# One step of the token mixing ahead of the last projections, and three of the last four normed blocks written by ScalarE

## The chip, the cores and the metric

The kernel runs on one core of a Trainium2 chip. The metric is the device time of one launch in microseconds (us). The engines are TensorE (PE in the profile, with PEld for its weight loads), VectorE (DVE), ScalarE (ACT), GpSimd (POOL) and SyncE (SP), whose queue issues nearly all DMAs.

## The reference

The sequence has S = 2048 tokens of width D = 512, in bfloat16. First an attention block with 32 heads of width 16 and a causal window of 256 tokens, then a token mixing: an MLP that runs along the sequence, with F = 1792 hidden units. Both are modulated by six vectors made from a condition `c`. Cut to what matters:

```python
sa, ca, ga, sb, cb, gb = split((silu(c) @ w_mod), 6)
h = layernorm(x) * (1 + ca) + sa
x = x + ga * (attention(h, wqkv) @ wo)         # sliding window
h = layernorm(x) * (1 + cb) + sb
h = layernorm(h)
u = gelu(einsum('bsd,sf->bdf', h, w1) + b1)    # contracts over tokens
y = einsum('bdf,fs->bds', u, w2) + b2
x = x + gb * transpose(y)
```

Because the first mixing product contracts over tokens, every one of its outputs needs the twice normed rows of all 2048 tokens.

## The kernel before

The 2048 rows are 16 row blocks of 128 tokens (`tb`, 0 to 15), in four groups of four. The kernel has three stages.

The first stage is the attention, which lasts to about 163 us of the span. Its work is a set of tasks on all engines, put in order at build time by a planner (class `Order`) from a list of ranks (`PLACE`) and estimated costs; the order of each engine's instructions is then fixed. In it the output projection and both layernorms of row blocks 0 to 11 are done too, giving `hb[0]` to `hb[11]`, and as a filler a part of the first mixing product: for the ten chunks of 128 hidden units in `PART` (4 to 13) the sums over row blocks 0 to 7 are made, and copied from PSUM to SBUF as `part[fc]` (L1177, on DVE, from one of two PSUM banks `bk`). The half of w1 for row blocks 0 to 7 is in SBUF (`w1a`) by then.

The second stage, the tail, is the one that the change touches. It is written out by hand inside `tc.manual_schedule()`, so that each engine runs its instructions in the order of the code (L1249 to L1297). It makes row blocks 12 to 15:

- `t_wo(tb)`: the projection, four matmuls into a bank `pa` of the pool `ps_big` (two banks, the ones that `bk` had), and the addition to the residual on DVE (L1255, L1259).
- `t1(tb)`: statistics for the first layernorm, `t_stats`: two DVE operations (`stats_of`, L447 and L448), then two on POOL for one over the standard deviation (`rstd_of`, L440 and L442).
- `t2(tb)`: the first layernorm applied (`t_apply`, L1268), times `bc_cb1` (L1279), plus `bc_sb` (L1280), all on DVE, and statistics of the result.
- `t3(tb)`: the second layernorm applied with `t_apply`, which writes `hb[tb]`.

The steps are skewed: in one pass of the loop the blocks 12 + step, 11 + step and 10 + step are at `t1`, `t2` and `t3`. Between the projections stand steps of the first mixing product: `emit_b1_group0_sc(sc)` adds row block `sc` to the hidden chunks 0 to 5, in six PSUM banks `pu0` and `pu1`, which are those that the attention's scores had. For `sc` below 8 that is four matmuls (chunks 4 and 5 have these rows in `part`), from 8 on it is six, with weights `w1b` (L1234). After the loop stand the remaining row blocks to 15. Row block `sc` needs `hb[sc]`.

`load_rest(done)` issues, on SP's queue, the eight loads of `w1b` (the other half of w1) and the fourteen of `w2r`; the first waits for the last matmul of the first projection in the tail, since it writes memory that the attention used.

The third stage is dense: hidden chunks 6 to 13 (L1318), Gelu on ACT (L1245, with an addition of `part` on DVE, L1243), the second mixing product (L1344) and the output (L1351, L1356, L1357).

Of the kernel before, what the change touches and what calls it, by code (L numbers as in the profile page):

```python
# [8 lines left out]
DT = mybir.dt  # L9
ACT = mybir.ActivationFunctionType  # L10
ALU = mybir.AluOpType

P = 128
# [5 lines left out]
NT = S // P  # L19
# [245 lines left out]
def kernel(  # L265
# [14 lines left out]
    nc = tc.nc  # L280
# [157 lines left out]
    def rstd_of(var, n, name):  # L438
        ve = small.tile([P, n], DT.float32, name=name + "_ve")
        nc.gpsimd.tensor_scalar(out=ve[:], in0=var, scalar1=EPS, scalar2=0.0, op0=ALU.add, op1=ALU.add)  # L440
        r = small.tile([P, n], DT.float32, name=name)
        nc.gpsimd.tensor_tensor(out=r[:], in0=ve[:], in1=mhalf[:, 0:n], op=ALU.pow)  # L442
        return r

    def stats_of(src, mv):
        stats = small.tile([P, nc.vector.BN_STATS_DIM], DT.float32, name="stats")
        nc.vector.bn_stats(out=stats[:], in_=src)  # L447
        nc.vector.bn_aggr(out=mv, in_=stats[:])  # L448
# [49 lines left out]
    with tc.manual_schedule():  # L498
# [26 lines left out]
        shift = small.tile([P, 1], DT.float32, name="shift0")  # L525
# [11 lines left out]
        for n, c0 in ((0, MF), (1, MO)):  # L537
            nc.scalar.activation(
                out=mask_q[:, 128 * n : 128 * n + 128].rearrange("p (a b) -> p a b", a=2),
                in_=rows[:, c0 : c0 + 64].unsqueeze(1).to_broadcast([P, 2, 64]), func=ACT.Copy,  # L540
# [78 lines left out]
        for par, lo, hi in ((0, 192, 512), (1, 0, 512), (0, 0, 192)):  # L619
            nc.vector.tensor_scalar(  # L620
                out=QP[0][:, par, lo:hi], in0=first[0][:, lo:hi], scalar1=mask_par[:, par : par + 1], scalar2=0.0,
                op0=ALU.mult, op1=ALU.add,
# [587 lines left out]
    def load_rest(after):  # L1210
        for sc in range(NT - NA):
            load = dma.dma_start(out=w1b[:, sc, :], in_=w1_v[:, NA + sc, :])
            if sc == 0:
                later_than(load, after)
        for fc in range(NF):
            dma.dma_start(out=w2r[:, fc, :], in_=w2_v[:, fc, :])

    def w1_of(sc, fc):
        w = w1box["a"][:, sc, :] if sc < NA else w1b[:, sc - NA, :]
        return w[:, fc * P : (fc + 1) * P]  # L1220
# [8 lines left out]
    def emit_b1_group0_sc(sc):  # L1229
        for gi, pu in ((0, pu0), (1, pu1)):  # L1230
            for i, fc in enumerate(fgroups[gi]):
                s0 = 8 if fc in PART else 0
                if sc >= s0:
                    nc.tensor.matmul(  # L1234
                        pu[:, i, :], lhsT=w1_of(sc, fc), rhs=hb[sc][:],
                        start=(sc == s0), stop=(sc == NT - 1),
                    )
# [11 lines left out]
    with tc.tile_pool(name="xp2", bufs=4) as xp2, tc.manual_schedule():  # L1249
        v = {}  # L1250

        def t_wo(tb):
            pa = ps_big.tile([P, D], DT.float32, name="pa")
            for g in range(ND):
                mm = nc.tensor.matmul(  # L1255
                    pa[:], lhsT=OT[12 + g][:, (tb - 12) * P : (tb - 11) * P], rhs=wod[:, g, :],
                    start=(g == 0), stop=(g == ND - 1),
                )
            nc.vector.tensor_tensor(out=xres[tb][:], in0=pa[:], in1=xres[tb][:], op=ALU.add)  # L1259
            return mm.ins.name  # L1260

        def t_stats(src, key):
            v[key] = xp2.tile([P, nc.vector.BN_AGGR_DIM], DT.float32, name="ln2_mv")
            stats_of(src, v[key][:])
            v[key, "r"] = rstd_of(v[key][:, 1:2], 1, "ln2")

        def t_apply(out, src, key):
            nc.vector.tensor_scalar(  # L1268
                out=out, in0=src, scalar1=v[key][:, 0:1], scalar2=v[key, "r"][:],
                op0=ALU.subtract, op1=ALU.mult,  # L1270
            )

        def t1(tb):
            t_stats(xres[tb][:], (2, tb))

        def t2(tb):
            h2 = v["h", tb] = xp2.tile([P, D], DT.bfloat16, name="h2")
            t_apply(h2[:], xres[tb][:], (2, tb))
            nc.vector.tensor_tensor(out=h2[:], in0=h2[:], in1=bc_cb1[:], op=ALU.mult)  # L1279
            nc.vector.tensor_tensor(out=h2[:], in0=h2[:], in1=bc_sb[:], op=ALU.add)  # L1280
            t_stats(h2[:], (3, tb))

        def t3(tb):
            t_apply(hb[tb][:], v["h", tb][:], (3, tb))

        for step in range(6):
            if step < 4:
                done = t_wo(12 + step)
                if step:
                    emit_b1_group0_sc(step - 1)  # L1290
                else:
                    load_rest(done)
            for f, n in ((t1, step), (t2, step - 1), (t3, step - 2)):
                if 0 <= n < 4:
                    f(12 + n)
        for sc in range(3, NT):
            emit_b1_group0_sc(sc)  # L1297

    ps_big.release()
# [28 lines left out]
    with tc.tile_pool(name="ftmp", bufs=3) as ftmp, tc.tile_pool(  # L1328
        name="ps_y0", bufs=4, space=PSUM
    ) as ps_y0, tc.tile_pool(name="ps_y1", bufs=4, space=PSUM) as ps_y1:  # L1330
        for tg in range(NT // 4):
# [16 lines left out]
            for tl, lo, hi in parts:  # L1348
# [3 lines left out]
                    out=o1[:, lo:hi], in0=pys[4 if lo else tl][:, lo:hi], scalar=b2FM[:, tb : tb + 1], in1=bc_gb[:, lo:hi],  # L1352
                    op0=ALU.add, op1=ALU.mult,
# [35 lines left out]
```

## Time and profile before

| | us |
|---|---|
| timed runs | 250.66, 251.11, 253.0 (median 251.11) |
| the profiled execution | 251.63 |
| its span, first to last instruction | 249.9 |
| busy: PE, DVE, ACT, POOL | 240.5, 168.1, 157.7, 125.2 |
| attention stage, about | 0 to 163 |
| tail, to the last L1234 | 163 to 184 |
| dense stage to the last matmul | 184 to 246.5 |

The profile has one row for each instruction or group, with its start, its duration, the engine, the line of the code, the tile written and the tiles read. In square brackets stands how long the engine was idle before it and what ended that idle time. "PE pa L1255 <- DVE part L1177" in the view of waits means that PE, at line 1255, waited for line 1177 on DVE. Matmuls overlap in the array: one of 512 columns is shown at 0.38 us, while their starts lie closer together, so the cost of a matmul is read from the distance of starts.

### The profile page before, as it was taken

To read this page: it belongs to the slowest core of one execution; us is meant where nothing else is said; L and a number is where in the kernel's file an instruction comes from. 1 tells how busy PE (TensorE), PEld (TensorE's weight loads), DVE (VectorE), ACT (ScalarE), POOL (GpSimd) and SP (SyncE) were. 2 spreads that over 40 slices of the span, in tenths; PEclk is the share of its full clock that TensorE was granted. 3 is DMA by queue.
4 is the path that set the end of the run, shared out by engine and by line. 5 is a ranking of instruction groups with operands and counts; after the bars stand their busy time and mean duration, and the time that the engine had idled before them with its cause. 6 is when DMAs were issued, how large, how long until landed. Compare 5 with 4: busy or idle time off the path is not lost.

```text
span 249.9 us, 10602 instructions
## 1 busy us (share of the span) xinstructions
PE 240.5 (96%) x4710; PEld 126.5 (51%) x4710; DVE 168.1 (67%) x324; ACT 157.7 (63%) x183; POOL 125.2 (50%) x228
## 2 busy tenths in 40 slices
PE   8999999989999999999999999989999999999994
PEld 2644745545654555655554664544444444444443
DVE  7686879869997978787958686679824404251544
ACT  5467999999999999999999999200056300000000
POOL 5536952980299999869894997724400000000000
PEclk9999999999999999999999999999999999999999
DMA  6935554332460444211201010059999000201121
GB/s 202 325 106 152 149 140 137 108 76 77 121 201 3 97 121 114 74 34 23 42 10 37 18 22 3 3 164 390 415 410 384 6 0 5 81 28 56 42 88 42
DMA packets 25490, 28.14 MB, mean 113 GB/s; under 512 B 10212, under 2 KB 22628, under 8 KB 25444
## 3 DMA queue, kind: packets, MB, share of 16 engines
q1 hardware_dynamic: 25148, 27.20, 34.8%
q8 instruction: 37, 0.61, 1.0%
q10 hardware_dynamic: 296, 0.26, 0.3%
q14 instruction: 9, 0.07, 0.1%
HBM read 22.03 MB, written 2.10 MB: 97 GB/s over the span
## 4 chain that ended last, share of the span: by engine, by line
PE 72%; ACT 14%; DVE 5%; POOL 3%; DMA 3%; issue 2%; SPq 0%; ACTq 0%; POOLq 0%
PE py L1344 19%; ACT et L734 13%; PE bk L473 11%; PE bk L477 8%; PE pu L1234 7%; PE bk L759 6%; PE pu L1318 6%; PE pss L716 5%; PE bk L504 3%; PE pss L688 2%; PE pss L724 2%; PE pa L1255 1%; DMA VU<-V 1%; DMA x<-in_A_x_dram 1%; PE pss L697 1%
## 5 line engine op out<-in xcount | busy, mean ns | idle before, releaser
L734 ACT ACTIVATE et<-pss 128x1024 bf16<-128x1024 f32 x152 | 140.6, 1062 | 3.4 <-PE pss L724 3.3
L1344 PE MATMUL py<-guT,w2r 128*128 128x512 bf16 (+1 forms) x238 | 48.5, 367 | 0.0
L1344 PEld LDWEIGHTS <-w2r 128*128 128x128 bf16 x238 | 23.2, 98 | 25.4
L1351 DVE SCALAR_TENSOR_TENSOR o<-py,bFM,bc_gb 128x512 bf16<-128x512 f32 (+1 forms) x17 | 11.7, 717 | 30.5 <-PE py L1344 30.5
L781 POOL TENSOR_TENSOR merge<-t,zr 128x512 bf16<-128x512 f32 x16 | 17.4, 1084 | 19.4 <-DVE zr L777 19.4
L768 DVE STREAM_TRANSPOSE t<-bk 128x512 f32<-128x512 f32 x32 | 22.6, 710 | 6.6 <-PE bk L759 5.4
L716 PE MATMUL pss<-QP,KT 32*128 32x192 bf16 (+2 forms) x672 | 25.6, 236 | 0.9 <-ACT et L734 0.5
L913 POOL TENSOR_SCALAR QP<-QR,mask_par 128x512 bf16<-128x512 bf16 x30 | 21.6, 724 | 7.7 <-DVE QR L626 4.7
L716 PEld LDWEIGHTS <-KT 32*128 32x128 bf16 x672 | 13.4, 92 | 18.2 <-issue 14.0
L473 PE MATMUL bk<-h1T,wqkv 128*128 128x512 bf16 x76 | 20.4, 382 | 0.3 <-ACT h1T L602 0.3
L759 PE MATMUL bk<-et,V 128*32 128x64 bf16 (+2 forms) x704 | 19.3, 240 | 0.4 <-DVE V L933 0.3
L759 PEld LDWEIGHTS <-V 128*32 128x32 bf16 x704 | 14.7, 96 | 7.8 <-issue 4.2
L724 PE MATMUL pss<-mask_q,mask_k 32*128 32x64 bf16 (+2 forms) x496 | 18.3, 213 | 0.0
L1245 ACT ACT_TABLE_LOAD x1 | 1.3, 1283 | 26.0 <-issue 26.0
L1243 DVE TENSOR_TENSOR gelu_a<-pu,part 128x512 f32<-128x512 f32 x10 | 6.5, 687 | 11.5 <-PE pu L1318 8.7
L1124 POOL TENSOR_TENSOR h<-h,bc_sb 128x512 bf16<-128x512 bf16 x12 | 13.9, 1155 | 0.6
L1318 PE MATMUL pu<-hb,w1b 128*128 128x512 bf16 x64 | 14.0, 379 | 0.0
L724 PEld LDWEIGHTS <-mask_k 32*128 32x128 bf16 x496 | 13.3, 93 | 0.4
L933 DVE CAST V<-bk 128x512 bf16<-128x512 f32 x16 | 11.1, 691 | 3.5 <-PE bk L477 1.5
L477 PE MATMUL bk<-h1T,wqkv 128*32 128x512 bf16 x192 | 12.7, 382 | 0.0
L759 PE MATMUL bk<-et,VU 128*32 128x64 bf16 x448 | 11.8, 194 | 0.9 <-DMA VU<-V 0.9
L759 PE MATMUL bk<-et,VL 128*32 128x64 bf16 x512 | 12.2, 193 | 0.0
(138 smaller groups left out, 406.0 us busy)
## 6 DMA issues: line engine op xcount, KB each, us to landing
w2r<-in_B_w_dram SPq DMA_DIRECT2D x14, 512.0 KB, 10.2
w1a<-in_B_w_dram SPq DMA_DIRECT2D x16, 224.0 KB, 3.2
w1b<-in_B_w_dram SPq DMA_DIRECT2D x8, 448.0 KB, 7.2
wmod<-in_w_mod_dram SPq DMA_DIRECT2D x8, 256.0 KB, 3.0
out_dram<-otile SPq DMA_DIRECT2D x15, 128.0 KB, 1.7
x<-in_A_x_dram SPq DMA_DIRECT2D x14, 128.0 KB, 3.1
VL<-V SPq DMA_DIRECT2D x15, 96.0 KB, 2.8
VU<-V SPq DMA_DIRECT2D x27, 48.0 KB, 2.4
```

The costliest lines, as they stand in the source:

```text
L473: nc.tensor.matmul(out, lhsT=lhsT, rhs=rhs, start=start, stop=stop, skip_group_check=True)
L477: nc.tensor.matmul(out[cols, :], lhsT=lhsT[:, cols], rhs=rhs, start=start, stop=stop, tile_position=(0, 32 * j), skip_group_check=True,)
L716: mm(pss[j // 2][:, j % 2, c0 : c0 + nq], lhsT=keys(4 * tg + kb)[rows[j], :], rhs=QP[s][rows[j], par, q0 : q0 + nq], start=n == 0, stop=False,
L724: mm(pss[j // 2][:, j % 2, c0 : c0 + hi - lo], lhsT=mask_k[rows[j], 0:P], rhs=mask_q[rows[j], lo:hi], start=False, stop=n + 1 == len(masks ...
L734: e = nc.scalar.activation(out=et[:], in_=held.pop(("pss", u, a))[:], func=ACT.Exp, scale=SCORE_SCALE)
L759: nc.tensor.matmul(po[32 * j : 32 * j + 32, q0 : q0 + nq], lhsT=v(j), rhs=held["et", s, k, j // 2][:, j % 2, c0 : c0 + nq], start=n == 0, ...
L768: nc.vector.transpose(out=held["t2", s][:, par, :], in_=psum.pop(("po", s, par))[:])
L781: nc.gpsimd.tensor_tensor(out=m[:].rearrange("p (b a d) -> p a b d", a=2, d=DH), in0=t2v(s, 0, DH, DH), in1=held["zr", s][:].to_broadcast( ...
L913: nc.gpsimd.tensor_scalar(out=QP[s][:, par, :], in0=QR[s][:], scalar1=mask_par[:, par : par + 1], scalar2=0.0, op0=ALU.mult, op1=ALU.add,)
L1234: nc.tensor.matmul(pu[:, i, :], lhsT=w1_of(sc, fc), rhs=hb[sc][:], start=(sc == s0), stop=(sc == NT - 1),)
L1318: nc.tensor.matmul(pu[:, i, :], lhsT=w1_of(sc, fc), rhs=hb[sc][:], start=(sc == s0), stop=(sc == NT - 1),)
L1344: nc.tensor.matmul(pys[4 if lo else tl][:, lo:hi], lhsT=w2r[:, fc, tb * P : (tb + 1) * P], rhs=guT[fc][:, lo:hi], start=(fc == 0), stop=(f ...
```

## The change

Two things are changed in the tail.

One step of L1234, that of row block 0, is put ahead of the loop, so ahead of the first projection. The steps in the loop then go one row block further each (1, 2, 3 in place of 0, 1, 2), and the rest begins at 4. The number of matmuls is the same. `load_rest` stays behind the first projection.

For row blocks 12, 13 and 14, the second layernorm (key 3) is applied by ScalarE, as an `Identity` activation with scale r and bias -mean * r. The bias is made by two operations of 128 x 1 on GpSimd, right behind those of `rstd_of`. Block 15 is still written by VectorE.

```diff
+        def by_scalar(key):
+            return key[0] == 3 and key[1] < NT - 1
+
         def t_stats(src, key):
             v[key] = xp2.tile([P, nc.vector.BN_AGGR_DIM], DT.float32, name="ln2_mv")
             stats_of(src, v[key][:])
-            v[key, "r"] = rstd_of(v[key][:, 1:2], 1, "ln2")
+            r = v[key, "r"] = rstd_of(v[key][:, 1:2], 1, "ln2")
+            if by_scalar(key):
+                shift = v[key, "shift"] = xp2.tile([P, 1], DT.float32, name="ln2_sh")
+                nc.gpsimd.tensor_scalar(
+                    out=shift[:], in0=v[key][:, 0:1], scalar1=-1.0, scalar2=0.0, op0=ALU.mult, op1=ALU.add,
+                )
+                nc.gpsimd.tensor_tensor(out=shift[:], in0=shift[:], in1=r[:], op=ALU.mult)
 
         def t_apply(out, src, key):
+            if by_scalar(key):
+                nc.scalar.activation(
+                    out=out, in_=src, func=ACT.Identity, bias=v[key, "shift"][:], scale=v[key, "r"][:],
+                )
+                return
             nc.vector.tensor_scalar(
                 out=out, in0=src, scalar1=v[key][:, 0:1], scalar2=v[key, "r"][:],
                 op0=ALU.subtract, op1=ALU.mult,
...
+        for sc in range(1):
+            emit_b1_group0_sc(sc)
         for step in range(6):
             if step < 4:
                 done = t_wo(12 + step)
                 if step:
-                    emit_b1_group0_sc(step - 1)
+                    emit_b1_group0_sc(step + 0)
                 else:
                     load_rest(done)
             for f, n in ((t1, step), (t2, step - 1), (t3, step - 2)):
                 if 0 <= n < 4:
                     f(12 + n)
-        for sc in range(3, NT):
+        for sc in range(4, NT):
             emit_b1_group0_sc(sc)
```

## The prediction

> **What bounds the kernel now.** I read the page's busy shares first, then TensorE (PE) in stretches around the change, then its waits there, then the chain that ended last.
>
> ```profile
> span 249.9 us, 10602 instructions
> ...
> PE 240.5 (96%) x4710; PEld 126.5 (51%) x4710; DVE 168.1 (67%) x324; ACT 157.7 (63%) x183; POOL 125.2 (50%) x228
> ...
> core 0: us, PE busy (x) PEld busy (x) DVE busy (x) ACT busy (x) POOL busy (x), PEclk, DMA share, GB/s
> 162.65:163.42 0.77, 0.00 (x1) 0.00 (x1) 0.69 (x1) 0.00 (x0) 0.00 (x0) 1.00 0.00 0
> 163.42:184.13 20.71, 20.71 (x96) 9.38 (x96) 15.38 (x36) 0.12 (x1) 7.19 (x16) 1.00 0.91 349
> 184.13:197.95 13.82, 13.82 (x66) 6.24 (x65) 5.16 (x8) 8.69 (x13) 0.00 (x0) 1.00 0.69 275
> 197.95:246.50 48.55, 48.54 (x239) 23.14 (x237) 17.69 (x34) 1.33 (x2) 0.00 (x0) 1.00 0.12 41
> ```
>
> The third to fifth numbers of a stretch are busy times. PE stands still for the 0.77 us from 162.65 to 163.42, and from there to 246.5 it has no gap at all, at granted clock 1.00. ScalarE (ACT) is idle until 184, VectorE (DVE) is busy 15.38 of 20.71 us.
>
> ```profile
> PE pa L1255 <- DVE part L1177: 0.8, 1, 0.8
> ...
> 158.99 3.66 PE bk L477 x64
> ...
> 162.67 0.70 DVE part L1177
> ...
> 163.42 1.89 PE pa L1255 x8
> ```
>
> The first row is PE's only wait after 156 us, the others are from the chain in order of time. The last partial product of the first stage ends at 162.65; DVE copies its PSUM bank out; only then may the projection of block 12 (L1255) write that bank. That is the hole. Everything after it is a row of matmuls whose number the change leaves alone, so the end moves by what happens to the hole, unless an operand comes late.
>
> **Edit one: one step of L1234 ahead of the projections.** PE's order in the built kernel differs in one thing: four L1234 matmuls of row block 0 stand ahead of the first L1255, and each later step stands one place earlier. Nothing is added. These four write the PSUM banks of the score tiles, not the bank that DVE empties, and read a block and weights from long before.
>
> ```profile
> 162.55 0.10 PEld L1255 LDWEIGHTS <-OT 128*128 128x128 bf16 x1 [0.42 <-issue]
> ...
> 168.59 5.34 PE L1234 MATMUL pu<-hb,w1a 128*128 128x512 bf16 x24
> 173.77 10.52 PE L1234 MATMUL pu<-hb,w1b 128*128 128x512 bf16 x48
> 184.13 2.11 PE L1318 MATMUL pu<-hb,w1b 128*128 128x512 bf16 x9
> ...
> 154.19 3.78 ACT L734 ACTIVATE et<-pss 128x1024 bf16<-128x1024 f32 x4
> 184.01 1.28 ACT L1245 ACT_TABLE_LOAD   x1 [26.04 <-issue]
> ```
>
> The first weights of the next stage are already loaded at 162.55 to 162.65, so the four can start at 162.65. Their banks were last read by ACT's exponentials, which end at 154.19 + 3.78 = 157.97. A matmul step costs (184.13 - 173.77) / 48 = 0.2158 us, four cost 0.86: they fill the hole of 0.77 and push the projection from 163.42 to 162.65 + 0.86 = 163.51, 0.09 late. PE's total is unchanged, so all PE work from 163.51 on has the hole behind it: gain 163.42 - 162.65 = 0.77 us. Bounds: 0, if the four cannot start early, and 0.79, the wait as rounded in its row.
>
> What is late next: blocks 12 to 15 start 0.09 later while their consumers come 0.77 earlier. On the new clock the first w1b step (row block 8) begins at 173.00, and blocks 12, 13, 14, 15 (24, 30, 36, 42 steps on) are wanted at 178.18, 179.47, 180.77 and 182.06.
>
> ```profile
> 164.51 4.40 SPq L1212 DMA_DIRECT2D w1b<-in_B_w_dram  x8
> 169.02 15.52 SPq L1216 DMA_DIRECT2D w2r<-in_B_w_dram  x14
> ...
> DMA to landing us min/median/max: 4.7/7.2/8.3
> ```
>
> The w1b loads are released by the end of block 12's projection, so they too start 0.09 later, at 164.60. Even at the longest landing of the eight, 8.3, the first is there at 172.90, against 173.00; at 4.7, which I take, since it goes out with nothing ahead of it, at 169.3. Later ones are issued some 0.55 apart and wanted 6 x 0.2158 = 1.29 apart, so their margin only grows. Cost 0.
>
> **Edit two: three of the four last blocks written by ScalarE.** DVE loses three applies; GpSimd (POOL) gains three pairs of 128x1 operations (the shift); ACT gains three activations. No queue of DMAs is touched by it.
>
> ```profile
> 164.48 0.69 DVE L1259 TENSOR_TENSOR x<-pa,x 128x512 bf16<-128x512 f32 x1 [1.11 <-PE pa L1255]
> ...
> 168.04 0.42 DVE L1279 TENSOR_TENSOR h<-h,bc_cb 128x512 bf16<-128x512 bf16 x1
> ...
> 173.47 0.38 DVE L1268 TENSOR_SCALAR hb<-h,ln_mv,ln 128x512 bf16<-128x512 bf16 x1
> 173.76 0.69 DVE L1259 TENSOR_TENSOR x<-pa,x 128x512 bf16<-128x512 f32 x1
> ...
> 177.47 0.38 DVE L1268 TENSOR_SCALAR hb<-h,ln_mv,ln 128x512 bf16<-128x512 bf16 x1
> 177.77 0.41 DVE L1268 TENSOR_SCALAR h<-x,ln_mv,ln 128x512 bf16<-128x512 bf16 x1
> ...
> 179.86 0.18 DVE L448 BATCH_NORM_AGGREGATE ln_mv<-stats 128x2 f32<-128x6 f32 x1
> ...
> 181.10 0.41 DVE L1268 TENSOR_SCALAR hb<-h,ln_mv,ln 128x512 bf16<-128x512 bf16 x1 [0.76 <-POOL ln L442]
> ```
>
> On DVE, block 12's apply was worth 173.76 - 173.47 = 0.29 to what follows, block 13's 177.77 - 177.47 = 0.30, and block 14's nothing, because DVE then waited 0.76 for POOL anyway. With the 0.09 delay, DVE stands at -0.20 after the first removal and -0.50 after the second. Block 15 is then ready at 181.10 - 0.50 + 0.41 = 181.01, wanted at 182.06: 1.05 to spare. Without edit two it would be 181.60, still 0.46 early.
>
> ```profile
> 168.17 0.72 POOL L442 TENSOR_TENSOR ln<-ln_ve,mhalf 128x1 f32<-128x1 f32 x1
> ...
> 170.27 0.56 POOL L442 TENSOR_TENSOR ln<-ln_ve,mhalf 128x1 f32<-128x1 f32 x1
> ...
> 174.02 0.56 POOL L442 TENSOR_TENSOR ln<-ln_ve,mhalf 128x1 f32<-128x1 f32 x1
> 175.48 0.29 POOL L440 TENSOR_SCALAR ln_ve<-ln_mv 128x1 f32<-128x1 f32 x1 [0.90 <-DVE ln_mv L448]
> ...
> 178.02 0.57 POOL L442 TENSOR_TENSOR ln<-ln_ve,mhalf 128x1 f32<-128x1 f32 x1
> ...
> L442 POOL TENSOR_TENSOR ln<-ln_ve,mhalf 128x1 f32<-128x1 f32 x8 | 5.0, 622 | 0.7
> ...
> L468 POOL TENSOR_TENSOR fours<-fours 128x4 f32<-128x4 f32 x9 | 2.2, 240 | 0.7
> ...
> L602 ACT ACTIVATE h1T<-pss,modFM 128x512 bf16<-128x512 bf16 x1 | 0.8, 777 | 2.6 <-PE pss L579 2.6
> ```
>
> A shift pair costs between 2 x 0.24 (L468, the same multiply on a small tile) and 2 x 0.62 (L442, a power), plus some 0.16 between; I take 0.64, the nearer kind, and keep 1.40. An ACT apply costs 0.78 (L602: the same function with scale and bias from memory), and I allow 0.1 before it. Block 12: power ends 170.92, pair 171.56, ACT 172.44, wanted 178.18. Block 13: 174.67, 175.31, 176.19, wanted 179.47. Block 14: 178.59 - 0.20 = 178.39, 179.03, 179.91, wanted 180.77; with the dear pair 180.67, still in time. Behind block 13's pair on POOL waits block 15's first square root: it could begin at 175.48 - 0.20 = 175.28, and with the dear pair begins at 176.07 and ends by 177.16, while DVE wants it at 177.27. The built order shows one more wait, of the last L442 for ScalarE; even if that were for block 14's write, at 179.91 it is over before 180.00, when that L442 is due. Behind ACT's applies stand only the table load and the Gelus, which at 184.01 - 0.77 = 183.24 wait for PE as before. Edit two alone moves no end: worth 0, hidden behind the weights stream and block 15's spare time.
>
> The Trainium skill speaks against this edit in two places. "SBUF — State Buffer", section "SBUF: two separate sides", says that VectorE and GpSimd take a shared port pair exclusively, one operation blocking the other. The trace agrees: L442 took 0.72 at 168.17, beside L1279 with two SBUF inputs, against 0.56 at 170.27. By that rule every shift operation beside such a DVE operation waits it out; the first rival prices this from the rows. "ScalarE: Activation LUTs", section "Rules for kernel authors", would leave a multiply and add on VectorE; by the trace that is 0.78 against 0.38 per apply, and the spare time of block 14 pays it.
>
> **Sum.** The profiled execution took 251.63, of which 249.9 is the span. 251.63 - 0.77 + 0 + 0 = 250.86. It lies 0.52 above the median of the three timed runs (250.66, 251.11, 253.0), so against the median 251.11 - 0.77 = 250.3.
>
> **Rivals.**
>
> 1. *The hole moves to a late block.* POOL's pairs beside DVE, or the power behind them, make block 14 or 15 late. For: block 14 has only 0.86 to spare, 0.10 with the dear pair. Against: blocks 12 and 13 have 5.7 and 3.3, and to eat the whole gain block 14 would have to slip 0.86 + 0.77. L442 takes 0.72 - 0.56 = 0.16 more beside L1279 than alone; if both shift operations stretch so and the pair is dear, block 14 is 0.2 late: 250.5. All of the gain back: 251.1. Chance 0.07.
> 2. *The four don't fill the hole.* If the first L1234 waits for the same copy, projection and blocks come 0.86 late and PE ends as before: 251.1, no gain. Against: no wait stands on it in the built order, and its banks are free since 157.97. Chance 0.07.
> 3. *Slower: ScalarE's new instructions are not at hand.* The page has queues that carry instructions, sharing the DMA engines, and from 166 on these are full.
>
> ```profile
> q14 instruction: 9, 0.07, 0.1%
> ...
> w2r<-in_B_w_dram SPq DMA_DIRECT2D x14, 512.0 KB, 10.2
> ```
>
> If ScalarE's next instructions had to be fetched behind these loads when block 12 is due (171.66), at 10.2 us, as a w2r load, block 12 would be written at 182.64 instead of 172.44; PE would stand 4.5 us at row block 12: 251.1 - 0.77 + 4.5 = 254.8. It decides from a delay of 5.74 + 0.77 = 6.5 us. Against: ScalarE is idle from 157.97, with time to fetch before the loads start, and its built order has no table load ahead of the three. Chance 0.04.
>
> **How the numbers follow.** Forecast 0.80 at 250.3; rivals 0.07, 0.07 and 0.04; 0.02 for runs that scatter further than those shown. The range goes from the fastest run less the gain, 250.66 - 0.79 = 249.9, less 0.2 because three runs hardly show the fastest, to the profiled run without any gain, 251.6, and 0.1 on top: 249.7 to 251.7. One per cent, 2.5 us, is about what a measurement of this kernel tells from no change. Forecast and rivals 1 and 2 lie within it: 0.93. Slower: rival 3 and a scatter like the run at 253.0, 0.05. Faster: 0.02, there is no second hole to fill.
>
> **What would show it.** Right: four L1234 rows from 162.65, the projection at 163.5, no PE wait from there on, row block 8 at 173.0, L1318 at 183.4, L1344 at about 197.2; ScalarE applies near 171.7, 175.4 and 179.1 at 0.78 each; block 15 on DVE near 180.6. Wrong: a PE wait on ACT or DVE at L1234 between 178 and 183 (rival 1), the first L1234 after 163.4 (rival 2), a long idle stretch of ACT past 172 with its sources ready (rival 3), or a w1b step that waits for a DMA at 173.

## The result and the profile after

The changed kernel takes 249.78 us (median of 20 runs, 249.07 to 251.65) against 251.12 (20 runs, 249.96 to 253.0). The ratio is 0.9947, with a 95% interval of 0.9926 to 0.9968: 0.8 to 1.9 us less. Forecast were 250.3 and a gain of 0.77. All ratios leave out single executions that ran over 1.5% longer than the fastest of their kernel (one of the reordering alone, one of four steps on VectorE), and they need not equal the quotient of the two medians.

The chain in order of time, of the changed kernel (start, duration, what):

```profile
157.83 3.64 PE bk L477 x64
161.47 0.16 issue
161.62 0.81 PE pu L1234 x3
162.44 1.73 PE pa L1255 x8
164.16 0.86 PE pu L1234 x4
```

The copy by VectorE (L1177) no longer stands in the chain. The row "issue" with three matmuls behind it is a missing record of the first of four. In a second profile of the same kernel all four are there. Its PE rows, from the timeline (start, duration, engine, line):

```profile
158.98 3.64 PE L477 MATMUL bk<-hb,w1a 128*32 128x512 bf16 x64
...
162.55 1.04 PE L1234 MATMUL pu<-hb,w1a 128*128 128x512 bf16 x4
163.42 1.89 PE L1255 MATMUL pa<-wod,OT 128*128 128x512 bf16 x8
...
172.92 10.52 PE L1234 MATMUL pu<-hb,w1b 128*128 128x512 bf16 x48
183.28 7.07 PE L1334 MATMUL pu<-hb,w1b 128*128 128x512 bf16 x32
```

This execution reached the last filler 0.01 us from where the profile of before did (158.99), so the two can be laid over each other. The projection begins at 163.42 in both. The dense stage (L1318 before, now L1334) begins at 183.28, not 184.13: 0.85 us earlier, or 0.84 from the filler on. The dense stage itself is unchanged: to the end of the last matmul it lasts 62.4 us in the kernel before and in the changed one.

The second edit, in the first profile after: GpSimd's power and pair for block 14, with the VectorE operation beside the power, then ScalarE's three applies and VectorE's last one.

```profile
176.49 0.43 DVE L1293 TENSOR_TENSOR h<-h,bc_cb 128x512 bf16<-128x512 bf16 x1
...
176.62 0.71 POOL L442 TENSOR_TENSOR ln<-ln_ve,mhalf 128x1 f32<-128x1 f32 x1
177.40 0.19 POOL L1271 TENSOR_SCALAR ln_sh<-ln_mv 128x1 f32<-128x1 f32 x1
177.67 0.19 POOL L1274 TENSOR_TENSOR ln_sh<-ln_sh,ln 128x1 f32<-128x1 f32 x1
...
170.25 0.81 ACT L1278 ACTIVATE hb<-h,ln_sh,ln 128x512 bf16<-128x512 bf16 x1 [13.43 <-DVE ln_mv L448]
173.93 0.81 ACT L1278 ACTIVATE hb<-h,ln_sh,ln 128x512 bf16<-128x512 bf16 x1 [2.87 <-POOL ln_sh L1274]
177.90 0.81 ACT L1278 ACTIVATE hb<-h,ln_sh,ln 128x512 bf16<-128x512 bf16 x1 [3.16 <-POOL ln_sh L1274]
...
179.31 0.41 DVE L1282 TENSOR_SCALAR hb<-h,ln_mv,ln 128x512 bf16<-128x512 bf16 x1 [1.00 <-POOL ln L442]
...
182.13 8.15 PE L1334 MATMUL pu<-hb,w1b 128*128 128x512 bf16 x36
```

A row block of L1234 is six matmuls, 1.295 us, so PE wants block 15 at 182.13 - 1.295 = 180.84, block 14 at 179.54. The two are written by 179.72 and 178.71: 1.12 and 0.83 us early. The three activations queue without a table load: ScalarE's only one in the tail still belongs to the Gelus.

### The profile page after: what moved, and what is told of

It is laid out like the page before. It is cut to its first block, busy times and chain, and to the rows that moved or that the text cites. A ratio compares the mean times of both kernels' runs of the same rounds, so it can differ in the third digit from the quotient of the medians.

```text
span 247.9 us, 10575 instructions
## 1 busy us (share of the span) xinstructions
PE 235.4 (95%) x4673; PEld 125.3 (51%) x4710; DVE 167.1 (67%) x321; ACT 160.0 (65%) x186; POOL 126.7 (51%) x234
## 4 chain that ended last, share of the span: by engine, by line
PE 72%; ACT 14%; DMA 4%; issue 3%; DVE 3%; POOL 2%; SPq 1%; ACTq 0%
PE py L1360 19%; ACT et L734 14%; PE bk L473 11%; PE bk L477 9%; PE pu L1234 7%; PE bk L759 6%; PE pu L1334 6%; PE pss L716 5%; PE pss L688 2%; PE pss L724 2%; DMA x<-in_A_x_dram 2%; DMA VU<-V 1%; PE pa L1255 1%; PE pss L697 1%; POOL xn L451 1%
## 5 line engine op out<-in xcount | busy, mean ns | idle before, releaser
L1360 PE MATMUL py<-guT,w2r 128*128 128x512 bf16 (+1 forms) x234 | 48.3, 366 | 0.2
L1360 PEld LDWEIGHTS <-w2r 128*128 128x128 bf16 x238 | 23.3, 98 | 25.3
L473 PE MATMUL bk<-h1T,wqkv 128*128 128x512 bf16 x65 | 18.5, 382 | 1.0 <-issue 0.5
L1278 ACT ACTIVATE hb<-h,ln_sh,ln 128x512 bf16<-128x512 bf16 x3 | 2.4, 813 | 19.5 <-DVE ln_mv L448 13.4
L1334 PE MATMUL pu<-hb,w1b 128*128 128x512 bf16 x62 | 13.9, 379 | 0.1
L477 PE MATMUL bk<-h1T,wqkv 128*32 128x512 bf16 x192 | 12.7, 381 | 0.0
L906 DVE CAST QR<-bk 128x512 bf16<-128x512 f32 x14 | 9.6, 687 | 4.0 <-PE bk L473 2.8
L900 DVE CAST KT<-bk 128x512 bf16<-128x512 f32 x15 | 10.3, 686 | 2.7 <-PE bk L473 1.2
```

What stands on the lines that cost most here:

```text
L473: nc.tensor.matmul(out, lhsT=lhsT, rhs=rhs, start=start, stop=stop, skip_group_check=True)
L477: nc.tensor.matmul(out[cols, :], lhsT=lhsT[:, cols], rhs=rhs, start=start, stop=stop, tile_position=(0, 32 * j), skip_group_check=True,)
L1334: nc.tensor.matmul(pu[:, i, :], lhsT=w1_of(sc, fc), rhs=hb[sc][:], start=(sc == s0), stop=(sc == NT - 1),)
L1360: nc.tensor.matmul(pys[4 if lo else tl][:, lo:hi], lhsT=w2r[:, fc, tb * P : (tb + 1) * P], rhs=guT[fc][:, lo:hi], start=(fc == 0), stop=(f ...
```

## The experiments

All times of the tail below are from the first of the 64 L477 matmuls to the first matmul of the dense stage: 184.13 - 158.99 = 25.14 before, 182.13 - 157.83 = 24.30 in the changed kernel.

**The reordering alone.** Against the changed kernel:

```diff
-            return key[0] == 3 and key[1] < NT - 1
+            return False
```

> The reordering alone: one L1234 step ahead of the projections, all four last blocks still written by VectorE. Hole theory (the gain is the filled hole of 0.85 us from matmul start to matmul start, nothing else): from the first L477 of the last filler (64 in a row) to the first matmul of the dense stage 24.30 us, as in the changed kernel, against 25.14 before; no PE wait in the tail; block 15 written 0.46 us and block 14 0.34 us before PE wants them; time 0.85 below the kernel before. Rival (the ScalarE half carries the part of the measured 1.33 that the hole does not explain): 24.3 us plus a wait at L1234 near the last blocks, and a time 0.5 us above that of the changed kernel.

249.96 us (12 runs) against 250.66; ratio 0.9952 (0.9926 to 0.9977). PE in the tail:

```profile
157.84 3.64 PE L477 MATMUL bk<-hb,w1a 128*32 128x512 bf16 x64
...
182.14 4.05 PE L1334 MATMUL pu<-hb,w1b 128*128 128x512 bf16 x17
```

24.30 us. VectorE wrote block 14 at 179.21 and block 15 at 180.38, 0.34 and 0.47 us before PE wanted them. The reordering has the whole gain of the tail.

**The ScalarE half alone.** The order of the matmuls is put back:

```diff
-        for sc in range(1):
-            emit_b1_group0_sc(sc)
...
-                    emit_b1_group0_sc(step + 0)
+                    emit_b1_group0_sc(step - 1)
...
-        for sc in range(4, NT):
+        for sc in range(3, NT):
```

> ScalarE writes blocks 12 to 14, the order of the matmuls is that of before. Hole theory: the hole of 0.8 us stays, tail 25.14 us from the first L477 of the last filler to the dense stage, time as before within 0.3 us. Rival (the ScalarE half carries 0.5 us): 250.6 where before has 251.1.

251.28 us against 250.66; ratio 1.0018 (0.9994 to 1.0043). The tail is 184.99 - 159.85 = 25.14 again, with the same hole:

```profile
159.85 3.64 PE L477 MATMUL bk<-hb,w1a 128*32 128x512 bf16 x64
164.28 1.89 PE L1255 MATMUL pa<-wod,OT 128*128 128x512 bf16 x7 [0.79 <-DVE part L1177]
...
184.99 1.24 PE L1332 MATMUL pu<-hb,w1b 128*128 128x512 bf16 x5
```

Worth nothing by itself, as forecast.

**The other bank first.** The kernel before, with the two PSUM banks of the fillers kept, and handed to the projections in the order in which VectorE empties them:

```diff
-            pa = ps_big.tile([P, D], DT.float32, name="pa")
+            pa = bank((tb + 1) % 2)
```

> The order and the engines of before, but the projections take the two PSUM banks in the other order: block 12 the one that was emptied earlier, block 13 the one that VectorE empties last. Hole theory (the hole is the wait for that one bank): block 12's projection starts as soon as the last filler is through, block 13's 0.86 us later, when the copy has just ended (0 to 0.1 us of wait); tail 24.3 to 24.4 us, time 0.75 to 0.85 below before, without any reordering and with ScalarE idle. Rival (the hole is PE's own change from 32-column to 128-column matmuls, or the wait for the last transposed attention block OT, and the four L1234 matmuls only happen to fit in it): the hole stays, 25.1 us, time as before.

249.82 us against 250.66; ratio 0.9962 (0.9937 to 0.9987).

```profile
158.78 3.64 PE L477 MATMUL bk<-hb,w1a 128*32 128x512 bf16 x64
162.35 1.90 PE L1252 MATMUL bk<-wod,OT 128*128 128x512 bf16 x7
...
183.08 3.19 PE L1316 MATMUL pu<-hb,w1b 128*128 128x512 bf16 x13
```

The projection starts 3.57 us after the first L477, as the four L1234 matmuls do in the changed kernel, and the tail is 24.30. So the hole was the wait for that bank and nothing else: it can be filled with other work, or not be made.

**Two steps ahead, with and without ScalarE.** `range(2)` in the changed kernel, the later steps one further; then the same with all four blocks on VectorE (one execution, 250.09 us against a median of 250.77).

> The changed kernel with two L1234 steps ahead of the projections, not one. Hole theory: the hole is already full, a second step gains nothing; projections and blocks come 0.86 us later while PE wants them at the same time, so block 14, 0.83 us early in the changed kernel, becomes 0.03 to 0.15 late; tail 24.30 + 0.03 to 0.15 us, time as the changed kernel within 0.2. Rival (more independent work ahead is better, there is more to fill than the hole): a further gain of up to 0.8 us.

> Two L1234 steps ahead of the projections, and all four last blocks written by VectorE (no ScalarE half). Spare-time theory (the ScalarE half is only cover: it brings blocks 14 and 15 earlier by about 0.5 us, which counts only where they would be late): block 14, 0.34 us early with one step ahead, is 0.52 us late with two, so PE waits about 0.5 to 0.6 us for VectorE at row block 14 of L1234, and the tail from the first L477 of the last filler to the dense stage is 24.30 + 0.5 to 0.6 = 24.8 to 24.9 us, against 24.39 with the ScalarE half. Rival (spare times read from the profile are not reliable to 0.3 us, or the ScalarE half is worth nothing anywhere): 24.4 us as with it.

With ScalarE the tail is 181.86 - 157.47 = 24.39 (249.53 us against 250.66; ratio 0.9969, 0.9944 to 0.9994): no second hole, and block 14 is 0.09 late. Without it the tail is 182.59 - 157.72 = 24.87:

```profile
171.66 7.93 PE L1234 MATMUL pu<-hb,w1b 128*128 128x512 bf16 x35
180.01 2.75 PE L1234 MATMUL pu<-hb,w1b 128*128 128x512 bf16 x12 [0.41 <-DVE hb L1282]
182.59 7.72 PE L1334 MATMUL pu<-hb,w1b 128*128 128x512 bf16 x34
```

PE waits at row block 14, 36 matmuls into the row (35 are recorded), for VectorE. From start to start the hole is 180.01 - (171.66 + 36 x 0.2158) = 0.58; the bracket says 0.41, since a matmul's row reaches past the point where the next may start. So the ScalarE half is worth 0.48 us, in this kernel and not in the changed one.

**Four steps ahead, with and without ScalarE.** `range(4)`, the later steps three further.

> Four L1234 steps ahead of the projections, with the ScalarE half. Spare-time theory: blocks come 3 x 0.863 = 2.59 us later than in the changed kernel, block 14 had 0.83 us to spare, so PE waits 1.76 to 1.85 us for ScalarE at row block 14; tail 24.30 + 1.8 = 26.1 us, slower than before (25.14) by 0.9 us; the w1b loads, released 2.59 us later, still land in time if the first takes the shortest landing of 4.3 us. Rival (the first w1b load takes the longest landing of 8.5 us): a wait of 2.7 us for a DMA at row block 8, and none at row block 14; tail 27.0 us.

> Four L1234 steps ahead of the projections, all blocks written by VectorE. Spare-time theory: block 14 is 2.25 us late (0.34 - 2.59), PE waits 2.25 to 2.35 us for VectorE at row block 14, tail 26.55 to 26.65 us; the time is 1.4 to 1.5 us above the kernel before and 2.3 above the changed kernel. Rival (DMA): a wait of 2.7 us at row block 8 in place of it, 27.0 us.

With ScalarE:

```profile
157.40 3.64 PE L477 MATMUL bk<-hb,w1a 128*32 128x512 bf16 x64
...
180.92 2.75 PE L1234 MATMUL pu<-hb,w1b 128*128 128x512 bf16 x12 [1.66 <-ACT hb L1278]
183.51 6.85 PE L1334 MATMUL pu<-hb,w1b 128*128 128x512 bf16 x30
```

26.11 us, the wait at row block 14, and none for a DMA. One execution took 251.09, the median of before 250.77: by the tail the gain is gone, and 0.97 more. Without ScalarE the expectation failed in the time, and in part in the place of the wait. PE's rows, and VectorE's writes of blocks 13 and 14:

```profile
172.62 6.64 PE L1234 MATMUL pu<-hb,w1b 128*128 128x512 bf16 x29
180.21 1.46 PE L1234 MATMUL pu<-hb,w1b 128*128 128x512 bf16 x6 [0.95 <-DVE hb L1282]
181.50 1.24 PE L1334 MATMUL pu<-hb,w1b 128*128 128x512 bf16 x5
182.69 2.54 PE L1234 MATMUL pu<-hb,w1b 128*128 128x512 bf16 x11
...
179.77 0.38 DVE L1282 TENSOR_SCALAR hb<-h,ln_mv,ln 128x512 bf16<-128x512 bf16 x1
...
182.26 0.38 DVE L1282 TENSOR_SCALAR hb<-h,ln_mv,ln 128x512 bf16<-128x512 bf16 x1
```

The first row is row blocks 8 to 12, 30 matmuls with one not recorded. So the wait in brackets is at row block 13, which VectorE finished at 180.15: from start to start it is 180.21 - (172.62 + 30 x 0.2158) = 1.12. Block 13 was 1.53 early with one step ahead (written by 176.72, wanted at 178.25 in the reordering alone), so three further steps, 2.59 us, had to make it 1.06 late; the expectation looked at block 14 alone. Block 14 was finished at 182.64 and wanted at 181.50, and row block 14 started 182.69 - 181.50 = 1.19 late. The two delays together are 2.31, near the 2.25 to 2.35 that I had worked out, and the last L1234 is through 185.28 - 158.68 = 26.60 us after the first L477, as expected.

PE did not stand still for all of it. The dense stage is not inside the part written out by hand, and in this build five of its matmuls were put ahead of row block 14: 5 x 0.2158 = 1.08 us of the second delay is work that is needed anyway. To the first matmul of the second mixing product (L1360) it is 198.01 - 158.68 = 39.33 us, against 38.12 in the reordering alone: a loss of 1.21, which is 2.31 less 1.08 but for rounding. 251.14 us (10 runs) against 250.77, ratio 1.0003 (0.9974 to 1.0032). What was tested here is therefore a little more than the number of steps.

**All four blocks on ScalarE.** In the changed kernel `return key[0] == 3`.

> All four last blocks written by ScalarE. Spare-time theory: behind the last power on GpSimd come the shift pair (0.46) and ScalarE's apply (0.81) in place of VectorE's 0.41; in the changed kernel a ScalarE apply ended 1.38 us after its power, so block 15 is ready at 178.72 + 0.56 + 1.38 = 180.66 on the clock of the changed kernel's profile, wanted at 180.84: no PE wait, tail 24.30 us. Rival (ScalarE's slower apply is on the path here): a PE wait of 0.3 us or more at row block 15.

One execution, 251.78 us against a median of 251.30. Tail 184.05 - 159.75 = 24.30, no PE wait. Block 15 is ready at 181.78 + 0.81 = 182.59 and wanted at 182.75: 0.16 us to spare.

**The changed kernel again.**

> The changed kernel once more, timed beside the kernel before on one chip. Scatter theory (the tail is worth 0.85 us, and what the first comparison showed beyond it, 1.33 in all, comes from where the clock stands when the first matmuls run and from stalls in the attention stage, which vary from run to run): ratio near 0.9966, between 0.994 and 0.999; tail again 24.30 us, but start and attention stage of another length than in the first profile. Rival (0.5 us more are gained somewhere in each run): ratio near 0.9947 again, and a profile that is shorter outside the tail.

250.30 us (12 runs) against 251.30; ratio 0.9959 (0.9928 to 0.999). The tail is 183.28 - 158.98 = 24.30, to the hundredth, but the span is 249.1, not 247.9. The parts of the profiles, but for the one whose tail is mixed with the dense stage (us; the attention stage starts with the first L473):

| profile | first L473 at | from there to the last filler | tail | span |
|---|---|---|---|---|
| before | 11.67 | 147.32 | 25.14 | 249.9 |
| changed | 10.37 | 147.46 | 24.30 | 247.9 |
| changed again | 10.80 | 148.18 | 24.30 | 249.1 |
| reordering alone | 10.51 | 147.33 | 24.30 | 247.9 |
| ScalarE alone | 10.37 | 149.48 | 25.14 | 250.8 |
| other bank first | 10.10 | 148.68 | 24.30 | 248.9 |
| two ahead | 10.37 | 147.10 | 24.39 | 247.6 |
| two ahead, VectorE | 10.09 | 147.63 | 24.87 | 248.4 |
| four ahead | 10.18 | 147.22 | 26.11 | 249.3 |
| all on ScalarE | 11.61 | 148.14 | 24.30 | 249.8 |

## Why the prediction was right

**What bounds: right.** PE is without a hole from the filler to the end in every kernel whose tail is 24.30. The kernels that were timed ten times or more have medians of 249.5 to 250.3 us where the tail is at most 24.39, and of 250.7 to 251.3 where it is 25.14 or, with four steps on VectorE, 1.21 above that of one step.

**Edit one: right in its mechanism, short in one term.** The term "the four can start at 162.65" came from the end of the last L477 row (158.99 + 3.66) and of the weight load shown there. They start at 162.55, on the same clock (changed again), 3.57 us after the first L477 where the row's end says 3.66. The hole was thus 163.42 - (158.99 + 3.57) = 0.86, not 0.77, and the four, at 0.86, fill it to 0.01: the projection was not pushed from 163.42 to 163.51 but stands at 163.42. That they fit so exactly is luck, since the hole was taken for 0.77. The gain of the tail is 25.14 - 24.30 = 0.84, above the upper bound of 0.79 that I had given.

**The spare times: right.** Forecast 1.05 for block 15 and 0.86 for block 14, found 1.12 and 0.83; without the ScalarE half 0.46 and, by the same working, 0.34, found 0.47 and 0.34. That is near enough to have foretold the waits of two and four steps ahead (0.09, 0.57 and 1.81 us of tail) from the profile, and, with block 13 counted too, the 2.31 of four steps without ScalarE. The w1b loads cost nothing even 2.6 us later.

**Edit two: worth nothing, right.** The pair cost 0.46 from start to end, less than the 0.64 I took, the apply 0.81, more than 0.78. The Trainium skill's advice in "ScalarE: Activation LUTs", section "Rules for kernel authors", to leave a multiply and add on VectorE holds for the single operation, as this trace shows (0.81 against 0.41 for block 15). It does not decide here: ScalarE was idle and VectorE's queue was the longer one (24.39 against 24.87 with two steps ahead).

**Rivals.** None came, but a part of the first one was met. Block 14's pair took 0.19 each and was not stretched; it fell beside L447, not beside the multiplication by `bc_cb1` (L1279 before, now L1293), so that case was not tested for the pair. The power ahead of it did fall beside L1293: it took 0.71, against 0.57 in the kernel before, and so 0.14 of block 14's spare time. Had GpSimd stood still until L1293 ended, at 176.92, the power would have come 0.30 later. The rows that the prediction read as agreeing with a full block thus show a smaller delay. ScalarE began its first apply 13.43 us after its last exponential and right behind the pair's end.

**Sum.** 251.11 - 0.77 = 250.3 against 249.78 measured, inside the range. The rest of the difference, 1.34 measured in all against 0.84 in the tail, is not from the change as far as these runs tell. The kernels with a tail of 24.30 gave ratios of 0.9947, 0.9952, 0.9962 and 0.9959; 0.84 of 251 is 0.9967, which lies in all four intervals, if in the first at its edge. The kernel before had medians of 251.12, 250.66, 250.77 and 251.30 in the four comparisons, and the first two columns of the table move by 1.6 and 2.4 us with an unchanged first stage. A further gain of a few tenths outside the tail can't be excluded, since all four ratios lie below 0.9967; but two steps ahead (0.9969, with 0.75 of tail) and ScalarE alone (1.0018, with none) show nothing of the kind. Why the attention stage varies was not followed up. So the mechanism and its size are shown by the tail, to 0.1 us; that the first comparison came out 0.5 us below the forecast is, as far as these runs tell, chance.

## What to carry to other kernels

Where the bounding engine has one hole, independent work that is needed anyway, put ahead of the waiting instruction, gained the hole and no more here; handing out the buffers in the order in which they come free gained the same here without moving anything. Before work is pulled ahead, read how early each later operand is, and not only the one with the least spare time: every further step costs that spare time, and past it the gain turns into a wait (0.84 gained with one step, 0.75 with two, 0.97 lost with four). Moving work to an idle, slower engine gained only where that spare time had run out.

## What the runs showed of the hardware

The first matmuls run at about half rate, and the moment at which that ends differs between executions. PE's rows, first of before, then of the changed kernel:

```profile
7.36 1.01 PE L504 MATMUL bk<-zero 128*128 128x512 bf16 x2
...
9.02 0.64 PE L504 MATMUL bk<-zero 128*128 128x512 bf16 x1
```

```profile
5.83 0.39 PE L504 MATMUL bk<-zero 128*128 128x512 bf16 x1
...
7.33 0.59 PE L504 MATMUL bk<-zero 128*128 128x512 bf16 x2
```

A row of two ends one distance of starts after the first has ended, so with 0.61 (at 6.49, before) and 0.38 (at 8.20, changed) for one matmul the starts lie 0.40 and 0.21 apart. The attention then starts at 11.67 and 10.37; over all profiles of the same first stage it is 10.09 to 11.67, a spread nearly twice the effect studied. The two latest, before and all on ScalarE, are the two that still show more than 0.6 for one matmul at 9 us. The granted clock is shown as 1.00 in these stretches too, so it does not tell of it. "TensorE: Matmul & The Clock Gate" of the Trainium skill, section "What's actually happening", has the window that opens the clock run free of the kernel's start, so that the point of change varies from run to run, by 0.5 us to either side. These rows agree that it varies, but by more: the change came before 5.83 us in one execution and after 9.02 in the other.

And a matmul's row ends after the next could start: the chain's row of the last filler lasts 3.66 us, while the next matmul started 3.57 after its first, 0.09 earlier. Holes on PE are better read from start to start.
